# An order of work around one batch change: second-layer weight differences and parts of batch 2's q and k ahead of batch 1's divisions, first-layer units as halves

## The chip, the cores and the metric

The kernel runs on one core of a Trainium2 chip. The metric is device microseconds (us) of one execution, as the median of a few timed runs; a lower number is better. Beside the timed runs there is one execution that was recorded by the hardware profiler, with its own time.

The engines are named as the profile names them: PE is the matrix engine (PEld is its weight load), DVE the vector engine, ACT the scalar engine with its table functions, POOL GpSimd, and SP the engine that issues nearly all DMAs. Each engine takes its instructions in the order in which the program has them; semaphores make one wait for another.

## The reference

Attention with a cosine-weighted ReLU feature map, and after it a two-layer network with a leaky ReLU:

```python
def phi(x, c, s):                       # c, s: cos and sin of pi/2 * position / S
    r = np.maximum(x, 0.0)
    return np.concatenate([r * c, r * s], axis=-1)
q_p, k_p = phi(q, cos_w, sin_w), phi(k, cos_w, sin_w)
kv  = np.einsum('bhsf,bhsd->bhfd', k_p, v)
z   = np.sum(k_p, axis=2)
num = np.einsum('bhsf,bhfd->bhsd', q_p, kv)
den = np.einsum('bhsf,bhf->bhs', q_p, z)[..., None] + 1e-06
x   = (num / den)                       # then (B*S, H*D)
h   = x @ w_in
g   = np.maximum(0.01 * h, h)
out = g @ w_out
```

Shapes: 8 batches, 8 heads, 576 positions, head dimension 64; w_in is 512 x 2048, w_out 2048 x 512; all inputs and the output are float32. The kernel computes in float16 with float32 sums.

## The kernel before, in words

**Tiling.** A batch's first 512 positions make one group of tokens (groups 0 to 7, one for each batch); the last 64 positions of all eight batches together make group 8. A group passes through these steps. `q_part` and `k_part` (both through `phi_half`, L239 on ACT and L241 on DVE) write the cosine or the sine half of phi(q) into `qp` and of phi(k) into `kpm` (main positions) and `kpt` (tail). `v_main` and `v_tail` cast v to float16 (`vmain`, `vtail`). `kv_all` or `kv_half` multiply phi(k) with v on PE (`kv_mm`: L290 main, L299 tail) and copy the result from PSUM to the tile `kv`; a column of ones beside v gives the denominator in the same product. phi(q) is transposed (`qpT`), by a DMA on SP's queue from batch 2 on. `num` (L381), or `num_half` (L417) for batches 0 and 1, multiplies it with `kv`; `divide` (L392 `den`, L396 `rden`, L397 `xs` or `xp`, all on DVE) divides and so frees the PSUM tile. The quotient is transposed on PE (`x_transpose` L446, `x_transpose_half` L434) and copied by ACT to `xT` (L447, L438). Then come the two layers of the network.

**The network.** Group 0 runs plain products (`ffn1`, `ffn2`). Group 1 runs its first layer plain, as units of two row blocks `m` (`f1_half` for the first units, `f1_pair` for the others, both through `f1_mm`, L496, four matmuls for each m), each pair ended by a leaky ReLU on ACT (L756). From group 2 on the first layer, and from group 1 on the second, use seven products of half blocks in place of eight, which need sums and differences of the operands: `w1_sums`, `w2_sums` (of the weights, made once; tiles `wb` and, in place, `w`), `x_sums`, `g_sums` (of the activations; tiles `gs`), all on DVE (L252 and L255). The second layer is L883.

**What sets the order.** The start, up to the first units of group 1, is written out by hand, statement by statement. What follows is a list of entries (`put(position, function, arguments)`) that is sorted by position and then issued; positions come from tables: `AT` for each batch's steps, `ENG` for the engine of each, `W2_AT` for the weight differences, `G1_AT` for the sums of group 1's activations. PE's stretch here is the seam between the two parts: the last products of group 0's second layer, batch 1's `kv_half` and `num_half`, group 1's first layer in units, and between the units batch 2's `kv_all`, `num` and `x_transpose`.

**Buffers.** PSUM pool "n" holds one tile (two banks): batch 2's four `num` follow each other in it, so each waits until the division of the one before has read it; `kv_all` uses it too, and so does the unit m = 2, 3 of group 1. Pool "o" holds two tiles, taken in turn by group 0's second layer and then by the transposes. After group 1's first layer the banks of "h" and "o" are given to the pools of the seven-product scheme (`open_banks`), where `ps_o0` and `ps_o1` (shown as ps_o) take the place of pool "o": the first second-layer product of group 1 therefore waits until ACT has copied batch 2's third transpose out of that bank.

**DMA.** All loads stand on SP's queue in a fixed order: q, k, v of batch 2 are issued early; then the four stores of group 0's output, the four transposes of batch 2's phi(q), then the load of batch 3's q, then its k and v. A transpose of phi(q) is issued when both halves of its `qp` are written.

Of the kernel before, what the change touches and what calls it, by code (L numbers as in the profile page):

```python
# [18 lines left out]
def kernel(  # L19
# [14 lines left out]
    nc = tc.nc  # L34
# [4 lines left out]
    MAIN = J * P  # L39
# [40 lines left out]
    ACT, DVE, POOL = nc.scalar, nc.vector, nc.gpsimd  # L80
# [152 lines left out]
    kv = [const.tile([P, H, NE], dt.float16, name=f"kv{b}") for b in range(B)]  # L233
# [11 lines left out]
    def copy(eng, o, i):  # L245
        if eng is ACT:
            nc.scalar.copy(o, i)
        else:
            eng.tensor_copy(o, i)
# [65 lines left out]
            ps.rearrange("p a (h e) -> p a h e", h=4)[:, :, :, 0 : NE - 1],  # L315
        )

    def kv_half(b, hg, where, blanks=0):
        ps = psum(where, [P, MAIN], dt.float32, "ps_kvh")
        idle(blanks, ps)  # L320
        ps = ps[:, 0 : 4 * NE]
        kv_mm(b, hg, ps)
        nc.scalar.copy(
            kv[b][:, 4 * hg : 4 * hg + 4, 0 : NE - 1],
            ps.rearrange("p (h e) -> p h e", h=4)[:, :, 0 : NE - 1],
        )
# [81 lines left out]
    def num_half(g, jp, hg, where, blanks=0):  # L408

        if hg == 0:  # L410
            st["xp", g, jp] = qppool.tile([P, 2, H, D], dt.float16, name="xp", tag="qp")
        ps = psum(where, [P, 2, 512], dt.float32, "ps_numh")
        idle(blanks, ps[:, 0])
        for o in range(2):
            for hh in range(4):
                h = 4 * hg + hh
                nc.tensor.matmul(  # L417
                    ps[:, o, hh * NE : (hh + 1) * NE - 1],
                    lhsT=st["qpT", g, 2 * jp + o][:, h, :],
                    rhs=kv[g][:, h, 0 : NE - 1],  # L420
                )
        divide(ps, st["xp", g, jp][:, :, 4 * hg : 4 * hg + 4, :])
# [44 lines left out]
        if m % 2 == 1 and chunks[-1] == NKC - 1 and hi == MAIN:  # L467
            nc.scalar.activation(st["g", g][:, m - 1 : m + 1, :], ps, AF.Lrelu)

    def ffn2(g, i, eng=DVE):  # L470
        tt, part = divmod(i, 4)
        if part == 0 and ("ps_o", g, tt) not in st:
            st["ps_o", g, tt] = psum("o", [P, DM], dt.float32, "ps_o")
        ps = st["ps_o", g, tt]
        for m in range(4 * part, 4 * part + 4):
            nc.tensor.matmul(
                ps,
                lhsT=st["g", g][:, m, tt * P : (tt + 1) * P],
                rhs=w2[:, m, :],
                start=(m == 0),  # L480
                stop=(m == NFT - 1),
            )
        if part == 3 and eng is not None:
            ffn2_out(g, tt, eng)
# [9 lines left out]
    def f1_mm(g, m, ps, chunks=range(NKC), lo=0, hi=MAIN):  # L494
        for c in chunks:
            nc.tensor.matmul(  # L496
                ps[:, lo:hi],
                lhsT=w1[m // 4][c // 2][:, c % 2, m % 4 : 512 : 4],
                rhs=st["xT", g][:, c, lo:hi],
                start=(c == 0 and lo == 0),  # L500
                stop=(c == NKC - 1 and hi == MAIN),
            )

    def f1_half(g, m, chunks, lo=0, hi=MAIN):

        if chunks[0] == 0 and lo == 0:
            st["h", m // 2] = psum("h", [P, 2, MAIN], dt.float32, "ps_h")
        for n in range(2):
            f1_mm(g, m + n, st["h", m // 2][:, n], chunks, lo, hi)

    def cast_w1(i, cp, eng, lo=0, hi=2):
# [190 lines left out]
    x_transpose_half(1, 1, 1)  # L702
# [40 lines left out]
                [P, NH, N2], dt.float16, name="g" + nm, tag="g" + nm, bufs=bufs  # L743
            )

    def f1_pair(g, m):

        early_ = m % NH < 2
        if m % 2 == 0 and not early_:
            st["h", m // 2] = psum("hn"[m == 2], [P, 2, MAIN], dt.float32, "ps_h")  # L750
        ps = st["h", m // 2]
        if not early_:
            f1_mm(g, m, ps[:, m % 2])
        if m % 2:
            up, u = divmod(m - 1, NH)
            nc.scalar.activation(  # L756
                st["gt", g][:, up, :, u : u + 2].rearrange("p h m n -> p m h n"),
                ps.rearrange("p m (h n) -> p m h n", h=2),
                AF.Lrelu,
            )  # L760
# [265 lines left out]
    def put(pos, f, *args):  # L1026
        line.append((pos, len(line), f, args))
# [47 lines left out]
    AT = {2: {'kc': (-12.0, -0.5, 13.0, 5.5, 13.0), 'ks': (-22.5, -12.5, -17.0, -10.5, 0.0), 'v': (11.0, 11.0, 12.5), 'kv': (16.5,), 'qc': (-8.0, 2.5, 4.5, 8.0), 'qs': (0.0, 4.5, 7.5, 13.0), 'qt': (6.0, 7.0, 8.0, 14.0), 'num': (19.0, 20.5, 24.0, 26.5), 'xt': (24.4, 24.9, 26.9, 30.9), 'xs': (35.5, 50.0, 36.0, 56.0)}, 3: {'load': (20.0, 24.0, 29.0), 'kc': (37.0, 42.5, 47.0, 49.0, 50.5), 'ks': (34.0, 43.5, 58.5, 50.5, 51.0), 'v': (56.0, 57.5, 59.0), 'kv': (62.0,), 'qc': (26.0, 28.5, 31.0, 33.5), 'qs': (31.5, 29.5, 41.0, 41.0), 'qt': (32.5, 34.5, 44.0, 53.0), 'num': (69.5, 76.0, 83.0, 89.0), 'xt': (89.5, 92.5, 93.0, 100.5), 'xs': (102.5, 106.0, 104.5, 113.5)}, 4: {'load': (-75.5, -104.5, -111.5), 'kc': (-80.0, -58.0, -55.0, -70.5, -49.5), 'ks': (-72.5, -54.5, -66.0, -55.0, -54.0), 'v': (-85.0, -40.5, -44.5), 'kv': (-37.5,), 'qc': (-72.5, -67.5, -50.0, -40.5), 'qs': (-65.5, -51.0, -43.5, -39.0), 'qt': (-52.0, -39.5, -33.0, -32.0), 'num': (-34.0, -28.3, -24.6, -16.4), 'xt': (-19.0, -16.8, -12.1, -8.4), 'xs': (-0.5, 0.0, 9.5, 16.5)}, 5: {'load': (-103.5, -85.5, -75.5), 'kc': (-64.5, -75.0, -78.0, -50.0, -49.0), 'ks': (-71.0, -59.0, -72.5, -60.5, -74.0), 'v': (-60.0, -52.0, -60.5), 'kv': (-46.5,), 'qc': (-87.0, -76.0, -44.5, -48.0), 'qs': (-72.5, -75.5, -44.0, -31.5), 'qt': (-55.0, -53.0, -43.5, -23.5), 'num': (-37.0, -32.3, -22.6, -15.9), 'xt': (-25.0, -14.8, -17.6, -8.9), 'xs': (-2.0, -2.0, -1.5, 5.0)}}  # L1075

    def loads(b, which):
        if which == 0:
# [14 lines left out]
    for s, at_ in W2_AT.items():  # L1093
        for i in range(2 - len(at_), 2):
            put(at_[i - 2], w2_sums, i, s)
    for s, at_ in G1_AT.items():
        for u in range(2):
            put(at_[u], g_sums, 1, s, 4 * u, 4 * u + 4)
# [6 lines left out]
    for b in range(2, NG):  # L1105
        at_, eng, s0 = AT[min(b, 5)], ENG[min(b, 5)], top[b] if b > 3 else 0
        if b < B:
            for n, pos_ in enumerate(at_.get("load", ())):
                put(s0 + pos_, loads, b, n)
            put(s0 + min(at_["kc"] + at_["ks"]) - 0.01, kp_tiles, b)  # L1110
            for j in range(J + 1):
                put(s0 + at_["kc"][j], k_part, b, j, 0, eng["kc"][j])
                put(s0 + at_["ks"][j], k_part, b, j, 1, eng["ks"][j])
            for n in range(3):
                put(s0 + at_["v"][n], v_part, b, n, eng["v"][n])
            put(s0 + at_["kv"][0], kv_all, b)
        else:
            for j in range(J):
                put(s0 - 100 + 3 * j, load_qtail, j)
        for j in range(J):  # L1120
            put(s0 + at_["qc"][j], q_part, b, j, 0, eng["qc"][j])
            put(s0 + at_["qs"][j], q_part, b, j, 1, eng["qs"][j])
# [37 lines left out]
```

## Time and profile before

| | us |
|---|---|
| timed runs | 272.84, 271.25, 272.84 (median 272.84) |
| the profiled execution, own time | 271.19 |
| its span, first to last instruction | 269.4 |
| PE busy | 263.5 (98% of the span) |
| PEld busy | 227.0 (84%) |
| DVE busy | 203.8 (76%) |
| ACT busy | 199.4 (74%) |
| granted PE clock, mean | 0.998 |

The time of the profiled execution lies 1.8 us above its span. Durations in a timeline row are those of the group; matmuls overlap, so the pace of a run of equal matmuls is read from the starts of neighbouring rows: four L496 matmuls of 128x512 take 0.87 us (217 ns each), one of 128x256 takes 0.109 us, eight of 128x65 about 0.26 us, four transposes of 128x128 about 0.22 us. On DVE and ACT too the next instruction starts a little before the one before it ends, and rows give that pace by their starts.

### The profile page before, as it was taken

The page shows a single profiled execution, that of the slowest core. Times are in us where ns is not written, and L with a number is a line of the kernel's source. Part 1 is how long each engine was busy: PE and PEld are TensorE (multiplying, and loading weights), DVE is VectorE, ACT ScalarE, POOL GpSimd, SP SyncE. Part 2 cuts the span into 40 slices and gives each one's busy share as a digit, 9 for nine tenths or more (in the row PEclk, how much of TensorE's full clock was granted, in tenths as well). Part 3 has the DMA queues.
Part 4 walks back from the last instruction along what each step waited for, and adds up shares of the span by engine and source line. Part 5 has one row for each costly group of instructions (what it writes and reads, how often), then busy time and mean ns, then how long its engine had stood idle before and what let it go on. Part 6 is the DMA issues. An engine that isn't in the chain of part 4 may idle for free.

```text
span 269.4 us, 6623 instructions
## 1 busy us (share of the span) xinstructions
PE 263.5 (98%) x2670; PEld 227.0 (84%) x2670; DVE 203.8 (76%) x452; ACT 199.4 (74%) x329; POOL 13.1 (5%) x25
## 2 busy tenths in 40 slices
PE   8999999999999999999999999999999999999994
PEld 6985455665998989899999999999999899999983
DVE  5875798797967898888879778977687758545652
ACT  8757476696888896978888788878877757666720
POOL 5047001000000000000000000000000000000000
PEclk9999999999999999999999999999999999999999
DMA  6999999979999979958995899669384412200324
GB/s 226 373 392 415 393 386 373 357 170 296 274 252 313 191 195 249 354 116 285 259 254 122 271 239 247 156 202 154 62 142 155 61 41 97 80 0 2 156 41 117
DMA packets 86190, 57.05 MB, mean 212 GB/s; under 512 B 55632, under 2 KB 81232, under 8 KB 85648
## 3 DMA queue, kind: packets, MB, share of 16 engines
q1 hardware_dynamic: 85584, 55.98, 77.0%
q8 instruction: 21, 0.34, 0.6%
q10 hardware_dynamic: 448, 0.39, 0.4%
q0 software_dynamic: 128, 0.26, 0.3%
q14 instruction: 9, 0.07, 0.1%
HBM read 36.70 MB, written 9.44 MB: 171 GB/s over the span
## 4 chain that ended last, share of the span: by engine, by line
PE 76%; DVE 2%; issue 0%
PE ps_o L883 33%; PE ps_h L782 30%; PE ps_h L496 4%; PE ps_num L381 3%; PE ps_h L883 3%; PE ps_kv L290 2%; DVE gs L255 0%; PE ps_kv L299 0%; PE ps_xt L446 0%; DVE xs L397 0%; DVE w L255 0%; DVE wb L255 0%; DVE ob L252 0%; DVE qp L241 0%; DVE kpt L241 0%
## 5 line engine op out<-in xcount | busy, mean ns | idle before, releaser
L883 PEld LDWEIGHTS <-g 128*128 128x128 f16 x648 | 62.7, 98 | 7.2 <-DVE g L252 0.3
L252 DVE TENSOR_TENSOR u<-ps_h,u 128x512 f32<-128x512 f32 x52 | 35.8, 688 | 21.0 <-PE ps_h L782 19.3
L883 PE MATMUL ps_o<-w,g 128*128 128x256 f16 x352 | 51.2, 273 | 0.0
L782 PEld LDWEIGHTS <-w 128*128 128x128 f16 x416 | 44.7, 113 | 1.2
L782 PE MATMUL ps_h<-xT,w 128*128 128x256 f16 x288 | 43.3, 273 | 0.0
L809 ACT ACTIVATE g<-u 128x1024 f16<-128x1024 f32 x26 | 27.5, 1058 | 11.2 <-DVE u L252 10.9
L802 ACT COPY u<-ps_h 128x512 f32<-128x512 f32 x52 | 30.5, 586 | 7.1 <-PE ps_h L782 7.0
L795 ACT ACTIVATE g<-ps_h 128x512 f16<-128x512 f32 x52 | 31.2, 602 | 5.6 <-PE ps_h L782 5.6
L782 PEld LDWEIGHTS <-wa 128*128 128x128 f16 x312 | 33.7, 113 | 1.2
L883 PE MATMUL ps_o<-wb,g 128*128 128x256 f16 x232 | 33.5, 273 | 0.0
L782 PE MATMUL ps_h<-xw,wa 128*128 128x256 f16 x208 | 31.3, 273 | 0.0
L883 PEld LDWEIGHTS <-gs 128*128 128x128 f16 x256 | 24.9, 98 | 2.9
L901 ACT COPY ob<-ps_o 128x512 f32<-128x512 f32 (+1 forms) x32 | 18.1, 565 | 11.9 <-PE ps_o L883 10.6
L496 PE MATMUL ps_h<-xT,w 128*128 128x512 f16 (+1 forms) x104 | 24.7, 363 | 0.0
L397 DVE TENSOR_TENSOR xs<-ps_num,rden 128x512 f16<-128x512 f32 x28 | 19.4, 691 | 1.0
L883 PE MATMUL ps_o<-w,gs 128*128 128x256 f16 x120 | 17.8, 273 | 0.0
L252 DVE TENSOR_TENSOR ob<-ps_o,ob 128x512 f32<-128x512 f32 (+1 forms) x22 | 14.9, 675 | 3.8 <-ACT ob L901 1.9
L883 PE MATMUL ps_o<-wb,gs 128*128 128x256 f16 x120 | 17.5, 273 | 0.0
L792 ACT COPY ps_h<-ps_h 128x512 f32<-128x512 f32 x26 | 14.9, 572 | 2.4 <-PE ps_h L782 1.5
L255 DVE TENSOR_TENSOR gs<-g 128x1024 f16<-128x1024 f16 x16 | 11.0, 688 | 7.3 <-ACT g L809 7.2
L782 PE MATMUL ps_h<-xw,w 128*128 128x256 f16 x104 | 15.6, 273 | 0.0
L782 PE MATMUL ps_h<-xT,wa 128*128 128x256 f16 x104 | 15.6, 273 | 0.0
(116 smaller groups left out, 411.8 us busy)
## 6 DMA issues: line engine op xcount, KB each, us to landing
qst<-in_q_dram SPq DMA_DIRECT2D x7, 1024.0 KB, 6.4
out_dram<-ob SPq DMA_DIRECT2D x14, 512.0 KB, 2.8
kst<-in_k_dram SPq DMA_DIRECT2D x6, 1024.0 KB, 7.1
vst<-in_v_dram SPq DMA_DIRECT2D x6, 1024.0 KB, 7.2
w1st<-in_moe_w_in_dram SPq DMA_DIRECT2D x8, 512.0 KB, 10.5
w2st<-in_moe_w_out_dram SPq DMA_DIRECT2D x4, 1024.0 KB, 12.3
kst<-in_k_dram SPq DMA_DIRECT2D x4, 512.0 KB, 8.1
vst<-in_v_dram SPq DMA_DIRECT2D x4, 512.0 KB, 8.3
```

The costliest lines, as they stand in the source:

```text
L252: nc.vector.tensor_tensor(out=o, in0=a, in1=b, op=ALU.add)
L255: nc.vector.tensor_tensor(out=o, in0=a, in1=b, op=ALU.subtract)
L381: nc.tensor.matmul(ps[lo:hi, h // 4, (h % 4) * NE : (h % 4 + 1) * NE - 1], lhsT=qpT[:, h, lo:hi], rhs=kv[b][:, h, 0 : NE - 1],)
L397: nc.vector.tensor_tensor(out=xs, in0=ps[:, :, 0 : 4 * NE].rearrange("p a (b e) -> p a b e", e=NE)[:, :, :, 0:D], in1=rden.rearrange("p (a ...
L496: nc.tensor.matmul(ps[:, lo:hi], lhsT=w1[m // 4][c // 2][:, c % 2, m % 4 : 512 : 4], rhs=st["xT", g][:, c, lo:hi], start=(c == 0 and lo == 0),
L782: nc.tensor.matmul(bank[:, p], lhsT=w(c), rhs=st["xb", g][n][:, c], start=(fresh and p == 0 and c == 0), stop=(c == 1), skip_group_check=True,
L792: nc.scalar.copy(bank1[bj], bank1[bi])
L795: nc.scalar.activation(st["g" + nm, g][:, 2 * t : 2 * t + 2], bank1[bi], AF.Lrelu)
L802: nc.scalar.copy(st["u", g, t][:, n], bank1[bi])
L809: nc.scalar.activation(st["gt", g][:, :, 1, 2 * t : 2 * t + 2], st["u", g, t], AF.Lrelu)
L883: nc.tensor.matmul(bank[..., lo:hi], lhsT=st[G2[n], g][:, m, pair * P : (pair + 1) * P], rhs=W2[n](m)[:, lo:hi], start=(fresh and m == 0), ...
L901: nc.scalar.copy(o_at(g, half_, col, pair), bank_of(bi, pair, pair is None))
```

## The change

The hand-written part: two of the four differences of w_out for the upper half (`w2_sums(1, 2)` and `w2_sums(1, 3)`, before in the list at positions 17.0 and 18.5) now stand around the output copy of group 0; the copy of `kv` of batch 1's second half of heads goes to DVE in place of ACT; batch 2's first q cosine part and first k sine part, before in the list, stand here, on DVE and on ACT; the first `num_half` of batch 1's second half of heads is set between the third and the fourth matmul of group 0's last product, and the second between the two halves of the first unit.

The list: group 1's units are issued as halves (two contraction blocks each), so that `kv_all`, the four `num` and the transposes of batch 2 can stand between halves; their positions move: `kv` from 16.5 to 15.5, `num` from (19.0, 20.5, 24.0, 26.5) to (17.5, 20.2, 23.2, 26.2), `xt` from (24.4, 24.9, 26.9, 30.9) to (23.1, 26.1, 29.2, 30.9). Batch 3's first q cosine part stays at 26.0. No instruction is added or removed on any engine.

```diff
-    def kv_half(b, hg, where, blanks=0):
+    def kv_half(b, hg, where, blanks=0, eng=ACT):
 ...
-        nc.scalar.copy(
+        copy(
+            eng,
             kv[b][:, 4 * hg : 4 * hg + 4, 0 : NE - 1],
 ...
-    def ffn2(g, i, eng=DVE):
+    def ffn2(g, i, eng=DVE, ms=range(4)):
 ...
-        for m in range(4 * part, 4 * part + 4):
+        for m in (4 * part + n for n in ms):
 ...
     nc.scalar.copy(st["xT", 1][:, 0:2, :], ps)
-    kv_half(1, 1, "n")
+    w2_sums(1, 2)
     ffn2_out(0, 0, DVE)
-    ffn2(0, 4 * 1 + 3, None)
+    w2_sums(1, 3)
+    kv_half(1, 1, "n", eng=DVE)
+    q_part(2, 0, 0, DVE)
+    ffn2(0, 4 * 1 + 3, None, (0, 1, 2))
+    num_half(1, 0, 1, "h")
+    ffn2(0, 4 * 1 + 3, None, (3,))
     ffn2_out(0, 1, ACT)
-    num_half(1, 0, 1, "h")
+    kp_tiles(2)
+    k_part(2, 0, 1, ACT)
+    f1_half(1, 0, range(0, 2), ns=(0,))
     num_half(1, 1, 1, "n")
-    f1_half(1, 0, range(0, 2))
+    f1_half(1, 0, range(0, 2), ns=(1,))
     x_transpose_half(1, 0, 1)
 ...
-    def f1_pair(g, m):
+    def f1_pair(g, m, part):
 ...
         if not early_:
-            f1_mm(g, m, ps[:, m % 2])
-        if m % 2:
+            f1_mm(g, m, ps[:, m % 2], (2 * part, 2 * part + 1))
+        if m % 2 and part:
 ...
     for n, m in enumerate(order):
-        put(2 * n, f1_pair, 1, m)
+        for part in range(2):
+            put(2 * n + part, f1_pair, 1, m, part)
 ...
-    W2_AT = {2: (17.0,), 3: (30.0, 18.5), 4: (75.5,)}
-    G1_AT = {3: (15.0, 31.0), 2: (17.5, 33.5), 1: (25.5, 39.5), 4: (63.0, 47.0)}
+    W2_AT = {(0, 3): 30.0, (1, 4): 75.5}
+    G1_AT = {3: (15.0, 31.0), 2: (17.7, 33.5), 1: (25.5, 39.5), 4: (63.0, 47.0)}
```

**DVE, between batch 1's divisions for the first and for the second half of heads** (`wb` and `w` are the weight differences, `osb` group 0's output, `kv` and `ps_kvh` batch 1's kv of its second half of heads). Before:

```order
L397 TENSOR_TENSOR xp<-ps_numh,rden 128x2x256
L249 COPY osb<-ps_o 128x512
L392 TENSOR_SCALAR den<-ps_numh 128x8
L396 RECIPROCAL rden<-den 128x8
L397 TENSOR_TENSOR xp<-ps_numh,rden 128x2x256
```

Now:

```order
L398 TENSOR_TENSOR xp<-ps_numh,rden 128x2x256
L255 TENSOR_TENSOR wb_218<-w_110,wb_217 128x1024
L249 COPY osb<-ps_o 128x512
L255 TENSOR_TENSOR w_110<-w_110 128x4x256
L249 CAST kv_204<-ps_kvh 128x4x65
L241 TENSOR_SCALAR qp<-qst,cos_t 128x8x64
L393 TENSOR_SCALAR den<-ps_numh 128x8
```

Four instructions stand ahead of the divisions that were not there.

**PE, where batch 2's kv begins** (`w_2_1` is the end of the unit m = 10, 11, `w_1_0` and `w_1_1` the unit m = 4). Before:

```order
L496 MATMUL ps_h<-xT,w_2_1_107 128x512
L496 LDWEIGHTS w_1_0_104
L496 MATMUL ps_h<-xT,w_1_0_104 128x512
...
L496 LDWEIGHTS w_1_1_105
L496 MATMUL ps_h<-xT,w_1_1_105 128x512
...
L290 LDWEIGHTS kpm
L290 MATMUL ps_kv<-vmain,kpm 128x65
```

Now:

```order
L497 MATMUL ps_h<-xT,w_2_1_107 128x512
L290 LDWEIGHTS kpm
L290 MATMUL ps_kv<-vmain,kpm 128x65
...
L299 MATMUL ps_kv<-vtail,kpt 128x2x65
L497 LDWEIGHTS w_1_0_104
L497 MATMUL ps_h<-xT,w_1_0_104 128x512
```

kv comes four matmuls of 128x512 earlier; those four now stand behind it.

**ACT, around batch 2's transposes** (`xT<-ps_xt` are the copies of the four transposes, `g` the leaky ReLU of group 1, `qp<-qst` parts of batch 3's q). Before:

```order
L447 COPY xT<-ps_xt 128x4x128 x2
L756 ACTIVATE g<-ps_h 128x2x2x256
L239 ACTIVATE qp<-qst,cos_t 128x8x64
L447 COPY xT<-ps_xt 128x4x128
L239 ACTIVATE qp<-qst,sin_t 128x8x64
```

Now:

```order
L448 COPY xT<-ps_xt 128x4x128
L239 ACTIVATE qp<-qst,cos_t 128x8x64
L448 COPY xT<-ps_xt 128x4x128
L764 ACTIVATE g<-ps_h 128x2x2x256
L448 COPY xT<-ps_xt 128x4x128
L239 ACTIVATE qp<-qst,sin_t 128x8x64
```

The first part of batch 3's q, which waits for that batch's load, has moved ahead of the second copy and of a leaky ReLU.

More of the change, by code (lines that the diff above doesn't have):

```diff
@@ L502, in f1_mm, with f1_half @@
             )
[L504 to L506 removed]
+    def f1_half(g, m, chunks, lo=0, hi=MAIN, ns=(0, 1)):
+        if chunks[0] == 0 and lo == 0 and ns[0] == 0:
             st["h", m // 2] = psum("h", [P, 2, MAIN], dt.float32, "ps_h")
[L508 removed]
+        for n in ns:
             f1_mm(g, m + n, st["h", m // 2][:, n], chunks, lo, hi)
@@ L744, in quarters @@
             )
-    def f1_pair(g, m):
+    def f1_pair(g, m, part):
         early_ = m % NH < 2
-        if m % 2 == 0 and not early_:
+        if m % 2 == 0 and part == 0 and not early_:
             st["h", m // 2] = psum("hn"[m == 2], [P, 2, MAIN], dt.float32, "ps_h")
@@ L1092 @@
         put(top[ALL - 1] + at_, w1_sums, 1, s, 2, 4)
-    for s, at_ in W2_AT.items():
-        for i in range(2 - len(at_), 2):
-            put(at_[i - 2], w2_sums, i, s)
+    for (i, s), at_ in W2_AT.items():
+        put(at_, w2_sums, i, s)
     for s, at_ in G1_AT.items():
@@ L1109 @@
                 put(s0 + pos_, loads, b, n)
-            put(s0 + min(at_["kc"] + at_["ks"]) - 0.01, kp_tiles, b)
+            if b > 2:
+                put(s0 + min(at_["kc"] + at_["ks"]) - 0.01, kp_tiles, b)
             for j in range(J + 1):
-                put(s0 + at_["kc"][j], k_part, b, j, 0, eng["kc"][j])
-                put(s0 + at_["ks"][j], k_part, b, j, 1, eng["ks"][j])
+                for part, nm in enumerate(("kc", "ks")):
+                    if at_[nm][j] is not None:
+                        put(s0 + at_[nm][j], k_part, b, j, part, eng[nm][j])
             for n in range(3):
@@ L1120 @@
         for j in range(J):
-            put(s0 + at_["qc"][j], q_part, b, j, 0, eng["qc"][j])
-            put(s0 + at_["qs"][j], q_part, b, j, 1, eng["qs"][j])
+            for part, nm in enumerate(("qc", "qs")):
+                if at_[nm][j] is not None:
+                    put(s0 + at_[nm][j], q_part, b, j, part, eng[nm][j])
             put(s0 + at_["qt"][j], q_transpose_dma, b, j)
```

2 lines of the change are left out of this document (1 added, 1 removed).

## The prediction

> **What bounds the kernel now.** I read the page first, then PE's timeline between 48 and 68 us, where all the moved work lies, then ACT, DVE and SP in the same stretch.
>
> ```profile
> PE 263.5 (98%) x2670; PEld 227.0 (84%) x2670; DVE 203.8 (76%) x452; ACT 199.4 (74%) x329; POOL 13.1 (5%) x25
> ```
>
> PE is busy for 98% of the span, and the change neither adds nor removes a matmul. So the time can only move by the waits of PE. A busy share hides small waits, so I take the starts of neighbouring rows:
>
> ```profile
> 48.47 0.67 PE L417 MATMUL ps_numh<-kv,qpT 128*128 128x65 f16 x16
> 48.98 1.03 PE L496 MATMUL ps_h<-xT,w 128*128 128x512 f16 x4
> 50.11 0.40 PE L434 MATMUL ps_xth<-ident,xp 128*128 128x128 f16 x4
> ...
> 57.50 0.67 PE L290 MATMUL ps_kv<-vmain,kpm 128*128 128x65 f16 x16
> 58.01 0.28 PE L299 MATMUL ps_kv<-vtail,kpt 128*128 128x130 f16 x2
> ...
> 58.75 1.02 PE L496 MATMUL ps_h<-xT,w 128*128 128x512 f16 x4
> 59.61 0.42 PE L381 MATMUL ps_num<-kv,qpT 128*128 128x65 f16 x8
> 59.87 1.03 PE L496 MATMUL ps_h<-xT,w 128*128 128x512 f16 x4
> 61.36 0.41 PE L381 MATMUL ps_num<-kv,qpT 128*128 128x65 f16 x8 [0.46 <-DVE xs L397]
> ...
> 64.04 1.03 PE L496 MATMUL ps_h<-xT,w 128*128 128x512 f16 x4
> 65.07 0.41 PE L381 MATMUL ps_num<-kv,qpT 128*128 128x65 f16 x8
> ...
> 67.50 0.71 PE L883 MATMUL ps_o<-w,g 128*128 128x256 f16 x5
> ```
>
> Four matmuls of 512 columns take 59.61 - 58.75 = 0.87 us. Then PE stands still three times. From 48.98 the four end at 49.85, and the transpose starts at 50.11: 0.26 us, for batch 1's division. From 59.87 they end at 60.74, and the second num starts at 61.36: 0.62 us, for batch 2's first division. From 64.04 they end at 64.91, and the fourth num starts at 65.07: 0.16 us, for the third division. That is 1.05 us, and it is all that the moved work can win: a gain of over 1% (2.7 us, about what a measurement of this kernel can tell from no change) is out of reach.
>
> **The divisions: what the change takes away.** The round from one num to the next is read here:
>
> ```profile
> 46.68 0.69 DVE L249 COPY osb<-ps_o 128x512 f32<-128x512 f32 x1 [0.68 <-PE ps_o L476]
> 48.93 0.17 DVE L392 TENSOR_SCALAR den<-ps_numh 128x8 f32<-128x8 f32 x1 [1.55 <-PE ps_numh L417]
> ...
> 49.36 0.69 DVE L397 TENSOR_TENSOR xp<-ps_numh,rden 128x512 f16<-128x512 f32 x1
> ```
> ```profile
> 60.52 0.69 DVE L397 TENSOR_TENSOR xs<-ps_num,rden 128x512 f16<-128x512 f32 x1
> ```
>
> From num to den 48.93 - 48.47 = 0.46, to the product 0.43, the product 0.69, and from its end (61.21) to PE 0.15: 1.73 us. Before, PE had between two nums 0.26 for the num and 0.87 of a half unit, 1.13 in all.
>
> First half wait (batch 1). DVE now does two differences of 1024 elements, at gs' 0.68 (quoted at the end; 0.61 from start to start) around the osb copy at 46.68; the first fits into its idle 0.68, the second runs from 47.29 to 47.89. Then comes the copy of kv, an operation that DVE does not show in this shape. Its bounds are 0.17 (the den row, 8 columns) and 0.69 (the osb row, 512 columns from PSUM); for 260 columns I take the middle, 0.43, so kv is there at 48.32 plus 0.06. ACT had it at:
>
> ```profile
> 48.03 0.39 ACT L323 CAST kv<-ps_kvh 128x260 f16<-128x260 f32 x1
> ```
>
> that is 48.42. PE now asks at 48.47 - 0.22 = 48.25, one matmul earlier, and waits 0.13 (0.39 with the upper bound, nothing with the lower). The Trainium skill, page VectorE: DVE Perf Modes, section Why PSUM operands drop a tier, says that a float32 operand in PSUM holds DVE to its plainest mode; by that the price grows with the columns as from den to osb, and the copy takes 0.43, while at the rate of DVE's SBUF operands the wait would be some 0.08 shorter. The osb row beside it, no faster than a two-operand product at 0.69, agrees with the page. From num at 48.38 the first xp ends at 48.38 + 0.46 + 0.43 + 0.69 = 49.96, and PE has 0.26 + 0.22 + 0.43 + 0.26 + 0.43 of work to 49.99: 0.03 of wait. So 0.16 stands against 0.26; PE leads by 0.10. The fourth instruction that DVE takes forward, batch 2's q cosine part, runs before den comes due at 48.84. It was work of the same engine before:
>
> ```profile
> 52.19 0.48 DVE L241 TENSOR_SCALAR qp<-qst,cos_t 128x512 f16<-128x512 f32 x1
> 52.59 0.48 DVE L241 TENSOR_SCALAR kpm<-kst,cos_t 128x512 f16<-128x512 f32 x1
> ```
>
> Its pace is 0.40, so DVE's queue behind the divisions is 0.40 + 0.10 = 0.5 earlier.
>
> Second and third wait (batch 2). Between nums there now stand 0.26 and six matmuls (1.31), 1.57 for the first and, with a transpose of 0.22, 1.79 for the others: against 1.73 that leaves 0.17, 0 and 0. So 0.78 becomes 0.17.
>
> **What it adds: kv behind ACT.** kv now starts four matmuls earlier, at 57.50 - 0.87 - 0.10 = 56.53, and its tail matmuls at 57.04. They need ACT's casts:
>
> ```profile
> 53.36 2.84 ACT L756 ACTIVATE g<-ps_h 128x1024 f16<-128x1024 f32 x3
> 56.07 1.06 ACT L247 CAST vmain<-vst 128x1024 f16<-128x1024 f32 x1
> 57.00 0.93 ACT L222 ACTIVATE vtail<-vtl,odd 128x256 f16<-128x256 f32 x2
> ...
> 58.95 0.59 ACT L313 CAST kv<-ps_kv 128x520 f16<-128x520 f32 x1
> ```
>
> The two vtail end at 57.93, and PE takes them at 58.01: before, this fitted by 0.08. A k part of 0.63 (like the q part further down) leaves this chain, but the third leaky ReLU cannot start before its unit. On PE that is issued by 57.50 - 3 x 0.87 = 54.89 and ends 0.16 later (a row of four ends at 1.03, not 0.87), at 55.05; the leaky ReLU started at 55.18 (53.36 and two paces of 0.91). With PE's lead of 0.10 and 0.06 to ACT it starts at 55.01, a gain of 0.17: then vmain at 55.91, vtail from 56.84 to 57.77, tail matmuls at 57.81. PE waits 0.77. The rest follows: kv's remaining 0.74 to 58.55, four matmuls to 59.42; ACT's kv copy, which before came 0.94 after the first tail matmul, runs from 58.75 to 59.34 and is just hidden. First num 59.42 (before 59.61), second 61.15, third 62.94, fourth 64.73, and with 1.31 and transposes of 0.22, and 0.44 between and behind them, the second layer at 67.62. Before it was 67.50. Up to here the waits are 0.16 + 0.77 + 0.17 = 1.10 against 1.05: **+0.1 us**, the gain spent on ACT's casts.
>
> **What it adds: batch 3's q in ACT's queue.** SP's timeline, the landing of that one load, and ACT's timeline:
>
> ```profile
> 53.80 5.95 SPq L347 DMA_TRANSPOSE qpT<-qp  x4
> 59.84 0.54 SPq L93 DMA_DIRECT2D qst<-in_q_dram  x1
> ```
> ```profile
> DMA to landing us min/median/max: 6.2/6.2/6.2
> ```
> ```profile
> 64.02 1.07 ACT L447 COPY xT<-ps_xt 128x512 f16<-128x512 f16 x2 [0.32 <-PE ps_xt L446]
> 65.11 1.02 ACT L756 ACTIVATE g<-ps_h 128x1024 f16<-128x1024 f32 x1
> 66.13 0.72 ACT L239 ACTIVATE qp<-qst,cos_t 128x512 f16<-128x512 f32 x1
> 66.76 0.57 ACT L447 COPY xT<-ps_xt 128x512 f16<-128x512 f16 x1
> ```
>
> The load is issued at 59.84 behind the four transposes and lands 6.2 us later, at 66.05; the q part starts at 66.13. No idle time shows in its row, because ACT had two copies and a leaky ReLU to do until 66.13. The third copy at 66.76 ends at 67.33, and PE needs it for the second layer at 67.50. In the changed order the q part stands ahead of the second copy, the leaky ReLU and the third copy. SP's transposes wait for DVE's sine part, which is 0.5 us earlier now, so I shift the whole of SP's row: load at 59.32, landed at 65.53, q part at 65.61. Then 0.63 for it, 0.48 for the second copy (half of the row's 1.07, less the overlap), 0.91 for the leaky ReLU, 0.57 for the third copy and 0.1 to PE: 68.30 against 67.62. PE waits **0.68 us**. What is late next is the last leaky ReLU, now behind the third copy (67.63), a q part and the fourth copy: 69.21 to 70.22. DVE's gs waits for it, and the x sums of group 2 stand behind gs:
>
> ```profile
> 68.96 0.68 DVE L255 TENSOR_TENSOR gs<-g,gs 128x1024 f16<-128x1024 f16 x1
> ```
>
> So gs is late by 1.3 us where PE is late by 0.8; of the 0.5 between, DVE's slack takes some or all. I put 0 to 0.4 on it and take 0.2.
>
> Bounds of the load: if the transposes don't move, the load lands at 66.05 still and the wait is 1.2; if it lands by 64.85, 5.5 us after the issue, there is none.
>
> **The sum.** 0.1 + 0.7 + 0.2 = +1.0 us: span 270.4, own time 271.19 + 1.0 = 272.2. The timed runs have two levels, 272.84 twice and 271.25 once, and the profiled execution is at the lower; with two of four at each I take their middle, 272.03, as the base: **273.0**.
>
> **The rivals.**
> *The load is early* (0.25): it lands by 64.85, the new order of ACT costs nothing, +0.1 remains, 272.1 (271.3 on the lower level), not slower. For it: fewer transposes in its way when it starts. Against it: 6.2 us for this load, and 0.7 earlier is needed.
> *The transposes don't move* (0.18): the wait is 1.2 and the x sums cost up to 0.4, so +1.7, 273.7. For it: the issue of the four took 5.95 us, as long as SP's queue lets it, whenever their halves are written. Against it: nothing else stands ahead of the first on SP.
> *The stalls go and nothing comes* (0.07): -0.6 to -1.0, 271.2 on the middle base. It needs ACT's vtail at 57.1, 0.7 earlier than its own rows give from the unit that they follow.
> *PE's clock drops* (0.02): two waits of 0.7 to 0.8 us stand 10 us apart. The start of the program shows what a slow clock costs:
>
> ```profile
> 1.09 5.33 PE L168 MATMUL ps_idle<-blank 128*128 128x256 f16 x28 [1.09 <-DVE blank L162]
> ```
> ```profile
> 61.00:63.00 2.00, 1.64 (x15) 1.06 (x16) 1.27 (x4) 0.32 (x1) 0.00 (x0) 1.00 0.77 178
> ```
>
> 28 matmuls of 256 columns took 5.3 us there, nearly twice the pace of 0.109 each. A stretch as long at half pace loses 2.3 us more: +3.3, 275.3. But in the window with the 0.62 wait the granted clock is 1.00. The Trainium skill, page TensorE: Matmul & The Clock Gate, section Part 1: The HAM clock gate, puts the drop at an idle window of about 3.4 us; by that rule waits of 0.8 don't reach it, and the trace agrees as far as 0.62 goes.
>
> **How the numbers follow.** The forecast, +0.6 to +1.4, has 0.48. The low end of the range is the first rival on the lower level, 271.2, with 0.3 for the faster case: 270.9. The high end is the second rival on the upper level, 272.84 + 1.7 = 274.5. Outside lie the clock, a part of the second rival and of the faster case. Faster by over 1% needs 2.7 us where 1.05 is to be had: 0.01. Slower by over 1% is the clock and a stall that I don't see: 0.04. The rest, 0.95, is within 1%, though more likely on its slower side.
>
> **What would show it.** In the changed profile: den after the first num of batch 2 about 1.7 us ahead of the second num, with no more than 0.2 us of wait; PE's L299 (there still L299) for batch 2 at 57.8 with a wait of some 0.8 for ACT's vtail; ACT idle ahead of its q part at about 65.6, and PE waiting 0.5 to 1.2 us for the copy of xT at the first matmul of the second layer (L891 there). I am wrong if the second layer starts by 67.5, or if the time moves by over 2 us either way.

## The result, and the profile after

| | median us | range us, runs |
|---|---|---|
| kernel before | 271.56 | 271.11 to 273.69, 22 |
| changed kernel | 273.31 | 272.26 to 274.51, 22 |

The ratio is 1.0046, with a 95% interval of [1.0031, 1.0062]: 1.25 us slower (0.84 to 1.69), under the 1% that the prediction calls no change. The forecast was +1.0 us and 273.0. The medians lie further apart, 1.75 us, since the runs of the kernel before stand on two levels, 14 of them at 271.1 to 271.9 and 8 at 272.4 to 273.7; their mean is 271.98, 1.28 below that of the changed kernel, and no profile shows what the upper level is.

PE still bounds everything, by the page of the profile and with the matmuls that it had. (DVE has one instruction more than before and ACT one less: the copy of `kv`.)

```profile
PE 263.8 (97%) x2670; PEld 226.6 (83%) x2670; DVE 204.3 (75%) x453; ACT 199.2 (73%) x328; POOL 13.1 (5%) x25
```

PE's timeline of the changed kernel (start, duration of the group, form, count, idle time before it and what ended it). Waits are read as in the prediction, from the starts of neighbouring rows:

```profile
46.94 0.61 PE L435 MATMUL ps_x<-ident,xp 128*128 128x128 f16 x8
...
48.04 0.81 PE L477 MATMUL ps_o<-w,g 128*128 128x512 f16 x3
48.82 0.42 PE L418 MATMUL ps_numh<-kv,qpT 128*128 128x65 f16 x8
...
55.91 1.24 PE L497 MATMUL ps_h<-xT,w 128*128 128x512 f16 x5
57.47 0.67 PE L290 MATMUL ps_kv<-vmain,kpm 128*128 128x65 f16 x16 [0.32 <-ACT vmain L247]
58.27 0.28 PE L299 MATMUL ps_kv<-vtail,kpt 128*128 128x130 f16 x2
...
60.13 1.46 PE L497 MATMUL ps_h<-xT,w 128*128 128x512 f16 x6
61.61 0.42 PE L382 MATMUL ps_num<-kv,qpT 128*128 128x65 f16 x8
...
66.93 0.59 PE L497 MATMUL ps_h<-xT,w 128*128 128x512 f16 x2
68.00 0.38 PE L447 MATMUL ps_xt<-ident,xs 128*128 128x128 f16 x4 [0.48 <-ACT xT L448]
68.22 0.59 PE L497 MATMUL ps_h<-xT,w 128*128 128x512 f16 x2
69.40 1.47 PE L891 MATMUL ps_o<-w,g 128*128 128x256 f16 x12 [0.58 <-ACT xT L448]
```

| place | before | predicted | measured |
|---|---|---|---|
| batch 1's divisions | 0.26 | 0.13 + 0.03 | 0.13 + 0.05 |
| kv behind ACT's casts | 0 | 0.77 | 0.48 + 0.30 |
| second num | 0.62 | 0.17 | 0.18 |
| fourth num | 0.16 | 0 | 0 |
| copies of xT, at the transposes and the second layer | 0 | 0.68 | 0.64 + 0.75 |
| sum | 1.05 | 1.8 | 2.53 |

(The 0.05 is from the starts 49.98 of two matmuls of 512 columns, which end at 50.42, and 50.47 of the transposes. Five matmuls of 512 columns take 1.08, so from 55.91 they end at 56.99, and kv starts at 57.47: 0.48. From 57.47 the sixteen take 0.51, as before, to 57.98, and the tail starts at 58.27: 0.30 by the single matmuls. Two of 512 columns take 0.43, so from 66.93 they end at 67.36, and the transposes start at 68.00: 0.64. From 68.22 they end at 68.65, and the second layer starts at 69.40: 0.75.) That is 1.48 us more waiting than before up to the second layer. The whole profile differs by 2.1 us in span, 271.5 against 269.4. Of that, 0.46 lies ahead of everything that was changed: the ps_x row (PE's transposes of batch 1's first half of heads) stands at 46.94 here and at 46.48 before, with the same code in front of it. This belongs to the single execution. Over the fourteen profiles of this case that row stands between 46.48 and 48.27, and one and the same kernel (the fifth and the tenth experiment) had 46.82 and 48.27. So kernels are compared from that row on. Without the start, this profile is 1.6 us longer than the one before, which is near the upper end of the 0.84 to 1.69 of the timed runs.

What ACT does ahead of the second layer, and what SP does for it, by their timelines:

```profile
66.76 0.72 ACT L239 ACTIVATE qp<-qst,cos_t 128x512 f16<-128x512 f32 x1 [1.90 <-DVE xs L398]
67.39 0.57 ACT L448 COPY xT<-ps_xt 128x512 f16<-128x512 f16 x1
67.85 1.03 ACT L764 ACTIVATE g<-ps_h 128x1024 f16<-128x1024 f32 x1
68.77 0.59 ACT L448 COPY xT<-ps_xt 128x512 f16<-128x512 f16 x1
```
```profile
53.75 6.55 SPq L348 DMA_TRANSPOSE qpT<-qp  x4
60.40 0.54 SPq L93 DMA_DIRECT2D qst<-in_q_dram  x1
```
```profile
DMA to landing us min/median/max: 6.3/6.3/6.3
```

The idle 1.90 us is put down to DVE's xs, but the q part reads nothing of it. It reads qst, and 60.40 + 6.3 = 66.7 is the landing of that load: it was the load that came last. Behind it on ACT stand the second copy, the leaky ReLU and the third copy, and the second layer follows at 69.40, 2.64 us behind the start of the q part.

The two waits do not touch the clock: between 66 and 70 us PE is busy for 2.94 of 4.00 us at a granted clock of 1.00.

```profile
66.00:70.00 4.00, 2.94 (x23) 1.72 (x21) 2.85 (x7) 3.24 (x6) 0.00 (x0) 1.00 1.09 360
```

The Trainium skill, page TensorE: Matmul & The Clock Gate, section Part 1: The HAM clock gate, puts the drop at an idle window of about 3.4 us; two waits of 0.64 and 0.75 us that lie 0.65 us apart agree with it.

### The profile page after: what moved, and what is told of

The parts are those of the page before. It is cut to its first block, busy times and chain, and to the rows that moved or that the text cites. A ratio compares the mean times of both kernels' runs of the same rounds, so it can differ in the third digit from the quotient of the medians.

```text
span 271.5 us, 6622 instructions
## 1 busy us (share of the span) xinstructions
PE 263.8 (97%) x2670; PEld 226.6 (83%) x2670; DVE 204.3 (75%) x453; ACT 199.2 (73%) x328; POOL 13.1 (5%) x25
## 4 chain that ended last, share of the span: by engine, by line
PE 91%; DMA 2%; ACT 2%; DVE 1%; issue 1%; POOL 1%; POOLq 0%; DVEq 0%
PE ps_o L891 33%; PE ps_h L790 30%; PE ps_h L497 6%; PE ps_h L461 5%; PE ps_o L477 5%; PE ps_num L382 3%; PE ps_h L891 3%; DMA ktl<-in_k_dram 2%; PE ps_kv L290 2%; PE ps_kvh L290 1%; PE ps_numh L418 1%; PE ps_qt L367 1%; PE ps_kv L299 1%; PE ps_xth L435 0%; DVE kpm L241 0%
## 5 line engine op out<-in xcount | busy, mean ns | idle before, releaser
L891 PEld LDWEIGHTS <-gs 128*128 128x128 f16 x256 | 24.9, 98 | 2.9
L891 PE MATMUL ps_o<-wb,gs 128*128 128x256 f16 x120 | 17.5, 273 | 0.0
```

The costliest lines, as they stand in the source:

```text
L891: nc.tensor.matmul(bank[..., lo:hi], lhsT=st[G2[n], g][:, m, pair * P : (pair + 1) * P], rhs=W2[n](m)[:, lo:hi], start=(fresh and m == 0), ...
```

## The experiments

**The theory**: the loss is batch 3's q part standing in ACT's queue ahead of the copies of xT while it waits for its load. **The rivals**: the copies would be late anyway (halves, later transposes), or the loss comes with the hand-written part and the start of the program.

**1. The q part behind the copies.** Edit of the changed kernel:

```diff
-'qc': (26.0, 28.5, 31.0, 33.5)      # batch 3
+'qc': (31.1, 28.5, 31.0, 33.5)
```

> The changed kernel, with one thing put elsewhere: batch 3's first q cosine part stands at 31.1 in the list instead of 26.0, behind the second, third and fourth copy of xT and the last leaky ReLU in ACT's queue. Theory (the loss is that q part standing ahead of the copies while it waits for its load): the two waits of 0.64 and 0.75 us before the second layer go, 1.4 us less than the changed kernel, so -0.2 to +0.2 us against the kernel before (ratio 0.999 to 1.001). What is left of waits up to there: 0.13 + 0.05 + 0.78 + 0.18 = 1.14 us. Rival 1 (the copies are late anyway, through the halves or the later transposes of x): PE waits at the same place and the ratio stays at 1.0046. Rival 2 (the start-up, 0.46 us later in the changed kernel's profile, is a part of the loss): 1.002, with PE's first ps_x row at 46.9 again.

Measured: 271.74, ratio 0.9992 [0.9982, 1.0003]. Its PE timeline has no wait at either place:

```profile
46.96 0.61 PE L435 MATMUL ps_x<-ident,xp 128*128 128x128 f16 x8
...
67.38 0.39 PE L447 MATMUL ps_xt<-ident,xs 128*128 128x128 f16 x4
67.61 0.59 PE L497 MATMUL ps_h<-xT,w 128*128 128x512 f16 x2
68.04 1.47 PE L891 MATMUL ps_o<-w,g 128*128 128x256 f16 x12
```

The start is as late as in the changed kernel (46.96), and the second layer is 1.36 us earlier. The whole loss is gone by one position in the list, and both rivals with it: the copies are not late without the q part, and the profiled execution that starts as late has an own time of 271.83, not the changed kernel's 273.42.

**2. The q part ahead of the copies, in the kernel before.**

```diff
-'qc': (26.0, 28.5, 31.0, 33.5)      # batch 3, kernel before
+'qc': (24.6, 28.5, 31.0, 33.5)
```

> The kernel before, with that one part put where the change puts it in ACT's queue: batch 3's first q cosine part at 24.6 instead of 26.0, between the first and the second copy of xT. Theory: ACT waits for the load at 66.05 while the second copy, a leaky ReLU and the third copy are queued behind it; from 66.13 on 0.63 + 0.48 + 0.91 + 0.57 + 0.1 gives the second layer at 68.8 in place of 67.5: +1.3 us (1.1 to 1.5), ratio 1.004 to 1.0055. Rivals 1 and 2: nothing, ratio 1.000 (0.999 to 1.001).

Measured: 272.52, ratio 1.0027 [1.0013, 1.0040]: +0.7 us, the sign of the theory and half of its size. ACT and PE in its timelines:

```profile
65.93 0.72 ACT L239 ACTIVATE qp<-qst,cos_t 128x512 f16<-128x512 f32 x1 [1.07 <-DMA qst<-in_q_dram]
```
```profile
68.58 1.47 PE L883 MATMUL ps_o<-w,g 128*128 128x256 f16 x12 [0.66 <-ACT xT L447]
```

Here the row names the load itself. The second layer stands at 65.93 + 2.65. But the load was 0.2 earlier than in the profile before and PE 0.26 later (ps_x at 46.74), so PE's wait was 0.82 and not 1.3. The price is what is missing between PE and the load in that execution, and not a fixed sum.

**3 and 4. The two parts of the change alone.** The third kernel has the new list (halves and positions) and the old hand-written part, the fourth the new hand-written part and the old list.

```diff
 # third kernel, against the changed one
-    w2_sums(1, 2)
     ffn2_out(0, 0, DVE)
-    w2_sums(1, 3)
 ...
-    W2_AT = {(0, 3): 30.0, (1, 4): 75.5}
+    W2_AT = {(1, 2): 17.0, (1, 3): 18.5, (0, 3): 30.0, (1, 4): 75.5}
 # fourth kernel, against the changed one
-            put(2 * n + part, f1_pair, 1, m, part)
+            put(2 * n, f1_pair, 1, m, part)
 ...
-'kv': (15.5,) ... 'num': (17.5, 20.2, 23.2, 26.2), 'xt': (23.1, 26.1, 29.2, 30.9)
+'kv': (16.5,) ... 'num': (19.0, 20.5, 24.0, 26.5), 'xt': (24.4, 24.9, 26.9, 30.9)
```

> Only the list part of the change (units as halves, kv, num and x transposes of batch 2 at the new positions); the hand-written part is that of the kernel before. Theory: waits of 0.26 (batch 1's division, as before), some 0.8 (kv behind ACT's casts), 0.17 (second num) and 1.15 to 1.3 (copies of xT behind the q part) = 2.4 to 2.5 us against 1.05 before: +1.3 to +1.5 us, ratio 1.005. Rival 2 (the loss comes with the hand-written part): +0.3 or less, 1.001.

> Only the hand-written part of the change (two differences of w_out, kv of batch 1 on DVE, batch 2's first q and k part, both num_half set into the matmuls); units whole and every position of the list as in the kernel before. Theory: waits of 0.13 + 0.05 (batch 1's division), 0.62 and 0.16 (batch 2's, as before) = 0.96 against 1.05 us: -0.1 us, ratio 0.9995 (0.9985 to 1.0005). Rival 2 (start-up and hand-written part): +0.4 us or more, 1.0015 or above, with PE's ps_x row at 46.9.

Measured: the list alone 273.45, ratio 1.0056 [1.0037, 1.0075]; the hand-written part alone 271.61, ratio 0.9997 [0.9986, 1.0009]. Both as the theory has it, so the loss lies in the list. In the third kernel's own profile, though, the waits were others than expected. This execution started 1.03 us late (ps_x at 47.51), so PE waited only 0.1 us at the second layer; and the third num waited 0.47 us for DVE, where in this kernel the second of the two differences stands ahead of that division:

```profile
64.59 0.42 PE L382 MATMUL ps_num<-kv,qpT 128*128 128x65 f16 x8 [0.30 <-DVE xs L398]
...
69.32 1.47 PE L884 MATMUL ps_o<-w,g 128*128 128x256 f16 x12
```

**5 and 10. kv's wait taken away, the q part left ahead.** What is the 0.78 us at kv worth, if PE waits for the load anyway?

```diff
-ENG 2: 'v': (ACT, DVE, ACT)
+ENG 2: 'v': (DVE, ACT, DVE)
-AT 2: 'v': (11.0, 11.0, 12.5) ... 'qc': (None, 2.5, 4.5, 8.0), 'qs': (0.0, 4.5, 7.5, 13.0), 'qt': (6.0, 7.0, 8.0, 14.0)
+AT 2: 'v': (11.0, 11.0, 13.5) ... 'qc': (None, 2.5, 4.5, 14.0), 'qs': (0.0, 4.5, 7.5, 14.1), 'qt': (6.0, 7.0, 8.0, 14.2)
```

> The changed kernel, with kv's wait made smaller and the q part left where the change has it: batch 2's first vmain cast and both vtail go to DVE, the second vmain cast stays on ACT, and batch 2's last q parts stand behind them (14.0 and 14.1, its transposes at 14.2). DVE gets 0.5 us more and puts off 0.8, so PE waits 0.1 to 0.3 us at kv in place of 0.78. Theory (the second layer cannot start before the landing of batch 3's q load plus 0.63 + 0.48 + 0.91 + 0.57 and some starts, 2.64 us in the three profiles that have this order): the 0.5 to 0.7 us go into the wait at the second layer, which grows from 1.38 to about 2, and the time is that of the changed kernel, ratio 1.0046 (1.003 to 1.006). Rival (PE's waits add up): -0.6 us, ratio 1.0025 or less.

> The kernel without kv's wait and with the q part left ahead, once more. It measured 1.0026 where the theory (kv's wait is swallowed by the wait for the load) gave 1.0046, but in its profile the load had landed at 65.31, not 66.69. If kv's wait is swallowed, this kernel and the changed one agree within 0.3 us wherever the load lands alike; if it counts, this one stays 0.5 us or more below the changed one of the same call (ratio 1.0026 against 1.0046).

For the tenth run, the changed kernel itself was measured beside it once more (the ninth):

> The changed kernel once more, beside the kernels of this call on the same chip: ratio 1.0046 (1.003 to 1.006). Theory: whatever the landing of batch 3's q load is in this execution, the second layer starts 2.64 us behind the start of the q part on ACT, and the waits at the x transposes and the second layer are what is missing to that.

Measured: first 1.0026 [1.0009, 1.0042], which spoke for the rival; the second time 1.0050 [1.0033, 1.0067], beside the changed kernel's 1.0040 [1.0026, 1.0055], measured with it. The tenth profile on PE:

```profile
48.27 0.61 PE L435 MATMUL ps_x<-ident,xp 128*128 128x128 f16 x8
...
58.31 0.67 PE L290 MATMUL ps_kv<-vmain,kpm 128*128 128x65 f16 x16
58.83 0.28 PE L299 MATMUL ps_kv<-vtail,kpt 128*128 128x130 f16 x2
...
69.84 1.47 PE L891 MATMUL ps_o<-w,g 128*128 128x256 f16 x12 [0.59 <-ACT xT L448]
```

kv waits for nothing in the tenth, and its start was 1.1 us later than the ninth's (47.17). Yet both come to the second layer at the same time, 69.82 and 69.84, since ACT's q part started alike behind the load, at 67.17 and 67.19. This alone does not show that kv's wait was swallowed. The late start was not swallowed: SP begins its first transpose 6.81 us behind ps_x in the ninth and 6.80 in the tenth. The loads went out alike (61.02 and 60.95) because the four issues took 1.16 us less in the tenth, which is luck as far as is known:

```profile
53.98 6.95 SPq L348 DMA_TRANSPOSE qpT<-qp  x4
```
```profile
55.07 5.79 SPq L348 DMA_TRANSPOSE qpT<-qp  x4
```

In both profiles of the kernel without kv's wait the load went out 12.7 us behind ps_x, in the two of the changed kernel 13.5 and 13.9. The edit also moves the q parts that the fourth transpose waits for; whether that shortens the issues is not shown. So the times of this kernel do not decide between theory and rival. (The fifth run was faster in its profile because its load landed at 65.3.)

What speaks for the theory is that the distance from the q part to the second layer does not change. In seven profiles with the q part ahead in which ACT waited for the load, the second layer follows the q part's start by 2.64 or 2.65 us, with a wait at kv or without, after an early start or a late one. They are the first seven rows; the last three have no such wait:

| kernel | q part starts | second layer | from ps_x to the second layer |
|---|---|---|---|
| changed | 66.76 | 69.40 | 22.46 |
| 2, before with q ahead | 65.93 | 68.58 | 21.84 |
| 3, list alone | 66.68 | 69.32 | 21.81 |
| 5, no wait at kv | 65.38 | 68.03 | 21.21 |
| 7, stores on POOL | 65.95 | 68.59 | 22.06 |
| 9, changed again | 67.17 | 69.82 | 22.65 |
| 10, as 5 | 67.19 | 69.84 | 21.57 |
| before | 66.13 | 67.50 | 21.02 |
| 1, q behind | 69.64 | 68.04 | 21.08 |
| 4, hand-written part alone | 66.88 | 68.35 | 20.89 |

**6. The load issued ahead of the fourth transpose.**

```diff
-AT 2: 'qt': (6.0, 7.0, 8.0, 14.0)
+AT 2: 'qt': (6.0, 7.0, 8.0, 20.1)
```

> The changed kernel, with batch 2's fourth q transpose moved behind the issue of batch 3's q load on SP (20.1 instead of 14.0); ACT's order is left as the change has it. Theory (it is the landing of the load that sets the second layer): the load is issued at about 59.06 in place of 60.40 and lands at about 65.4 in place of 66.69; second layer at 65.4 + 2.64 = 68.04, where PE asks at 68.01: the 1.38 us go nearly whole, ratio 1.000 (0.999 to 1.001). Rival 1 (the q part costs by its place in ACT's queue, whenever the load lands): 1.004 or more. Rival 2 (the load lands when the transfers ahead of it are through, whenever it is issued): landing at 66.3 or later, 1.003 or more.

Measured: 273.47, ratio 1.0047 [1.0033, 1.0061], which is no gain at all; the time by itself is what both rivals gave. SP (with the load's time to landing), ACT and PE in its timelines:

```profile
59.16 0.53 SPq L93 DMA_DIRECT2D qst<-in_q_dram  x1
59.80 2.32 SPq L348 DMA_TRANSPOSE qpT<-qp  x1
```
```profile
DMA to landing us min/median/max: 6.3/6.3/6.3
```
```profile
65.59 0.72 ACT L239 ACTIVATE qp<-qst,cos_t 128x512 f16<-128x512 f32 x1
...
67.48 1.02 ACT L764 ACTIVATE g<-ps_h 128x1024 f16<-128x1024 f32 x1 [0.70 <-PE ps_h L497]
```
```profile
49.62 0.42 PE L418 MATMUL ps_numh<-kv,qpT 128*128 128x65 f16 x8 [0.46 <-DVE kv L249]
...
66.58 0.43 PE L382 MATMUL ps_num<-kv,qpT 128*128 128x65 f16 x8 [0.46 <-DMA qpT<-qp]
```

The profile speaks against both rivals, since the load did as expected: issued at 59.16, landed 6.3 us later, and ACT then waited for PE and no longer the other way. But the fourth transpose now stood behind the load, its issue took 2.32 us, and the fourth num waited 0.63 for it. The other new wait, 0.62 at 49.62 where the changed kernel has 0.13, is this execution's. A load of batch 1's k came late, DVE was late with the divisions, and its kv copy, which now stands behind two differences there, came late with it; 0.23 more went within the ps_x row, which is 0.87 long in place of 0.61. Together these are 1.35, against the 1.39 that the load won. How often that k load comes late is not known, so this kernel's time is explained only in part.

**7. The stores off SP's queue.** The load goes out late because the issue of one transpose is held:

```diff
-        nc.sync.dma_start(out_rows(g)[:, tt, :], osb)
+        nc.gpsimd.dma_start(out_rows(g)[:, tt, :], osb)
```

> The changed kernel, with group 0's four output stores issued by POOL in place of SP. In six profiles the issue of a q transpose on SP takes 1.24 us, but one of the four takes 0.1 to 1.16 longer (1.16 in the changed kernel, 0.65 before, 0.1 where the first is issued a microsecond later). Theory a (it is held by the stores that stand ahead of it on SP's queue): four issues of 1.24 to 1.35 from 53.75, load issued at about 59.0 to 59.1, landing 65.3, and the wait at the second layer falls from 1.38 to 0.1, ratio 1.000. Theory b (it is held by the transposes' own transfers, or by transfers of other queues): load issued at 60.3 still, ratio 1.0046 as in the changed kernel.

Measured: 272.66, ratio 1.0027 [1.0014, 1.0039]. The transposes as a group (duration of one in ns as lowest, median and highest), here, in the changed kernel and in the kernel before:

```profile
L348 SPq DMA_TRANSPOSE qpT<-qp x4: 1231/1288/2362, 53.3 to 58.8; - x4
```
```profile
L348 SPq DMA_TRANSPOSE qpT<-qp x4: 1240/1296/2402, 53.8 to 59.1; - x4
```
```profile
L347 SPq DMA_TRANSPOSE qpT<-qp x4: 1241/1248/1897, 53.8 to 58.5; - x4
```

With no store on SP the longest issue is still 2.36, so theory a falls. What holds it stays open: other transfers, or the transposes' own. This kernel is 0.5 us faster than the changed one, though their intervals overlap. The hold does not explain it. In this one profile the load landed 5.7 us after its issue in place of 6.3, which would explain it; but the fifth run's load took 5.8 with the stores on SP, so that the stores are the reason is not shown.

**8, 12 and 11. Both repairs.** The q part behind the copies, kv's casts as in the fifth kernel, and one of the two differences back in the list, ahead of batch 2's first division; in the eleventh both.

```diff
-    w2_sums(1, 3)
 ...
-    W2_AT = {(0, 3): 30.0, (1, 4): 75.5}
+    W2_AT = {(1, 3): 16.0, (0, 3): 30.0, (1, 4): 75.5}      # 11: and (1, 2): 15.9
```

> The changed kernel with both repairs: batch 3's q part behind the copies of xT (31.1), batch 2's first vmain cast and both vtail on DVE, and the second of the two differences of w_out back in the list (16.0), so that DVE can cast batch 1's kv at once. Theory: of PE's waits there stay 0 (batch 1's kv), 0.05, 0.1 to 0.3 (kv), 0.18 (second num) and nothing at the second layer: 0.3 to 0.5 us against 1.05 before. -0.5 to -0.7 us against before, ratio 0.9975 to 0.998. Rival (the waits that go come back at the next load or copy): ratio 0.999 to 1.000, as with the q part behind alone.

> The kernel with both repairs and one difference of w_out moved back, once more, since its interval [0.9967, 1.0012] settled nothing: 0.9975 to 0.998 if the 0.75 us that its profile lacks in waits (0.27 against 1.05) are kept to the end, 0.999 to 1.000 if they are not.

> The kernel with both repairs (q part behind the copies, vmain and vtail on DVE), and now both differences of w_out back in the list, ahead of batch 2's first division: DVE has nothing but the output copy between batch 1's divisions, as before, so that a late load of batch 1's k (in one profile it came 1.3 us late, and PE waited 0.63 us for DVE's kv copy) finds 1.2 us of slack. Waits of PE in this stretch: 0 to 0.05, 0 (kv), 0.18 (second num) and 0: 0.2 against 1.05 before, so -0.6 to -0.8 us, ratio 0.997 to 0.998. Rival (the waits that go come back elsewhere): 0.999 to 1.000.

Measured: the eighth 271.33, ratio 0.9990 [0.9967, 1.0012]; the same kernel again, as the twelfth, 271.04, ratio 0.9981 [0.9970, 0.9992], which is 0.5 us faster than the kernel before and, by the ratios 0.9981 and 1.0040 measured together, 1.6 us faster than the changed one. The eleventh: 271.56, ratio 1.0000 [0.9988, 1.0012], where -0.6 to -0.8 us was expected. PE in the twelfth:

```profile
47.13 0.61 PE L435 MATMUL ps_x<-ident,xp 128*128 128x128 f16 x8
...
57.08 0.67 PE L290 MATMUL ps_kv<-vmain,kpm 128*128 128x65 f16 x16
57.59 0.28 PE L299 MATMUL ps_kv<-vtail,kpt 128*128 128x130 f16 x2
...
67.33 1.47 PE L890 MATMUL ps_o<-w,g 128*128 128x256 f16 x12
```

From ps_x to the second layer it takes 20.20 us, against 21.02 before: 0.82 less, by the waits at 0.04, 0.05 and 0.18. Of these 0.82, 0.5 (0.2 to 0.8) are seen in the time. And the eleventh, on DVE and on PE:

```profile
59.31 0.68 DVE L255 TENSOR_TENSOR w<-w 128x1024 f16<-128x1024 f16 x1
59.92 0.15 DVE L393 TENSOR_SCALAR den<-ps_num 128x8 f32<-128x8 f32 x1
```
```profile
59.31 1.46 PE L497 MATMUL ps_h<-xT,w 128*128 128x512 f16 x6
61.18 0.41 PE L382 MATMUL ps_num<-kv,qpT 128*128 128x65 f16 x8 [0.41 <-DVE xs L398]
```

The second difference on DVE there puts den off from 59.52 (0.46 behind the num at 59.06) to 59.92, and the wait at the second num is back at 0.57. There is room for one of the two, and not for both. This execution still comes from ps_x to the second layer in 20.60 us, 0.42 less than before; it loses 0.3 behind it, in PE's products after batch 3's last num, and why was not followed.

## Why the prediction was right, and where it was not

**The waits that go** were right to 0.02 us each: 0.13 + 0.05, 0.18 and 0. The price that the trace had not shown, the copy of kv on DVE, was put at 0.43 as the middle of two rows, and measured:

```profile
48.35 0.42 DVE L249 CAST kv<-ps_kvh 128x260 f16<-128x260 f32 x1
```

So a copy from PSUM took 0.17, 0.42 and 0.69 at 8, 260 and 512 columns, in step with the columns. The Trainium skill, page VectorE: DVE Perf Modes, section Why PSUM operands drop a tier, which holds a float32 operand in PSUM to the plainest mode, agrees with these.

**kv behind ACT's casts** was right in size: tail matmuls predicted at 57.81, measured at 58.27, less the 0.46 of the start 57.81. First num 59.42 predicted, 59.88 - 0.46 = 59.42. Of the place it had only a part. It put the whole wait at the tail matmuls, but 0.48 of it comes at the first kv matmul, which waits for vmain; by the prediction's own rows vmain ends at 56.97, behind kv's start at 56.53.

**The q part in ACT's queue** was the right mechanism, with the term mis-sized: 0.68 put down, 1.39 measured. (0.64 of it comes already at the fourth transpose, which waits for the second copy of xT; the prediction had all of it at the second layer.) The step that failed is "I shift the whole of SP's row": load at 59.32, landed at 65.53. The first half of it held, since SP began the first transpose at 53.75, that is 53.29 when the late start is taken off. But the four issues took 6.55 us in place of 5.95, and the load went out at 60.40, or 59.94 when the start is taken off: where it had been before, and a little later. That is the second rival's mechanism (the transposes don't move), for which the text had a wait of 1.2 us. The evidence against it there, that nothing else stands ahead of the first on SP, looked at the wrong place. It was the third that was held, as this row of SP's timeline has it, with the third from 56.55 and the fourth from 59.06, 2.5 us apart instead of 1.3:

```profile
56.55 3.75 SPq L348 DMA_TRANSPOSE qpT<-qp  x2
```

From the load on, the working was right: q part, copy, leaky ReLU, copy and 0.1 to PE were put at 2.69 (from 65.61 to 68.30) and measured 2.64.

**The form of the sum** was the other weak point. Waits of PE were added up to a price of the change, 0.1 and 0.7. The seven profiles of the table show that they don't add: with the q part ahead, the second layer stands at the landing plus 2.7, whatever PE waited for before. kv's 0.77 was not spent beside the 0.68; without it, by the same rule, the 0.68 would have grown. For the forecast this made no difference, because 68.30 came from the landing.

**The knock-on** through gs and the x sums was put at 0.2 and is there: from the second layer to the end it takes 271.5 - 69.40 = 202.1 us, against 201.9 before. gs starts 2.01 us behind the second layer instead of 1.46, and the sum `xw` 7.27 instead of 6.98, so that PE, through with its eight matmuls at 77.04, waits 0.11 for it:

```profile
76.17 1.04 PE L891 MATMUL ps_o<-wb,g 128*128 128x256 f16 x8
77.15 0.63 PE L790 MATMUL ps_h<-xw,wa 128*128 128x256 f16 x4
```
```profile
76.67 0.43 DVE L255 TENSOR_TENSOR xw<-xT,xw 128x512 f16<-128x512 f16 x1
```

**The forecast and the base.** The base of 272.03, the middle of two levels, is close to the mean of the 22 runs (271.98) and above their median of 271.56. That 273.0 came so near to the median of 273.31 is luck in part: a base too high made up for a term too small, and 271.56 + 1.0 would have been 272.6.

**The signs.** The prediction wanted den of batch 2 some 1.7 us ahead of the second num; by its own round of 1.73 less 0.46 it is 1.27, and 1.28 was measured (60.33 to 61.61). The others came, the q part later than said.

**The first rival** (an early load) did not come in any profile of the changed kernel: its load landed at 66.7 and 67.1. Nor did the clock.

## What to carry to other kernels

In a queue that runs in order, look at what an instruction that waits for a transfer is moved ahead of: here a part that nobody needed soon stood ahead of two copies that PE needed at once, only because the copies' positions had moved and its own had not. Where such a wait sets a stage's start, work out the time at which the stage can start (landing plus the chain behind it), and not a sum of waits; what is won ahead of it is worth nothing until it is out of the way, unless it brings the transfer itself forward. A transfer queued behind several others on one queue is not earlier because the first of them is.

## What the hardware showed that was not expected

The issue of a q transpose takes SP 1.24 us each, and it lands 2.7 to 2.8 us after its issue begins; but in most profiles one of the four took longer, up to 2.40 and, in the changed kernel's second profile, 2.80:

```profile
L348 SPq DMA_TRANSPOSE qpT<-qp x4: 1241/1296/2797, 54.0 to 59.7; - x4
DMA to landing us min/median/max: 2.9/4.7/5.3
```

The third kernel, which sent its first at 54.82, had no issue over 1.34, but the tenth, which sent it at 55.07, had one of 1.71, so a late start is not what avoids it. Moving the stores to another queue did not change the hold. The start of the program, with the same code, came to the same matmul within a spread of 1.8 us from execution to execution, more than the whole effect of this change.
